# One activation table for Ln and Exp, loaded once ahead of the gated scan

## The chip, the cores and the metric

The kernel runs on one core of a Trainium2 chip. The metric is the device time of one execution in microseconds. Engines: TensorE (PE in the profile), VectorE (DVE), ScalarE (ACT), GpSimd (POOL) and SyncE (SP), each with an instruction stream of its own, in order; they wait for each other by semaphores.

## The reference

A complex gated linear recurrence over 768 steps, for 4 batches of 8 heads with 48 channels, and behind it a mixture of 8 experts in which each token takes one.

```python
mag = np.sqrt(a_re * a_re + a_im * a_im)
scale = np.minimum(mag, 0.999) / (mag + 1e-06)
a_re_n, a_im_n = (a_re * scale, a_im * scale)
for t in range(S):
    ar, ai = (a_re_n[:, :, t, :, None], a_im_n[:, :, t, :, None])
    kv = np.einsum('bhd,bhe->bhde', k[:, :, t], v[:, :, t])
    S_re, S_im = (ar * S_re - ai * S_im + kv, ar * S_im + ai * S_re)
    y[:, :, t] = np.einsum('bhd,bhde->bhe', q[:, :, t], S_re)
...
logits = x @ w_gate + modality_bias[modality_id]
e_idx = np.argmax(logits, axis=1)
out[mask] = gate_w[mask, None] * (np.maximum(x[mask] @ w1[e], 0.0) @ w2[e])
```

## The kernel before

The kernel has two parts. `gate_loop` computes the recurrence and the router's logits, `moe_sorted` (line 196 on) sorts the tokens by expert and computes the experts in 31 tiles of 128 tokens.

`gate_loop` cuts the 768 steps into 8 groups of L = 96 and puts (batch, head, group) on 128 partitions, so that the work comes in two rounds of two batches each (`NR = 2`). For each round there are two functions.

`elem(r)` works element by element, in 12 chunks of T = 8 steps, from the last step of a group to its first. A chunk loads the gates into `ab` (lines 65 and 66), squares them on ScalarE (L68), adds the squares on VectorE (L70), and turns the sum into the inverse magnitude by Ln (L72) and Exp (L73) on ScalarE. L75 (ScalarE) and L76 (VectorE) make the normalised gate's factor `g`, L79 (VectorE) with L80 and L81 (ScalarE) the table `an`, and L84 and L85 are the eight steps of the backward product of gates, each two VectorE instructions that depend on the ones before. From these products in `A`, ScalarE takes squares (L93), VectorE their sum (L95), ScalarE again Ln (L96) and Exp (L97). VectorE scales `q` by that (L98, L100) and `k` (L101); the scaled `k` goes to `kh` in DRAM (L102), the scaled `q` through eight transposes on TensorE (L106) into PSUM, and ScalarE copies them, four at a time, into `QT` (L107). The program interleaves neighbouring chunks: on each engine the second half of a chunk (L93 on) stands beside the first half of the next one (L68 to L81).

`units(r)` reads `kh` back as `KW` (L132) and runs the 8 groups in order, two batches each: transposes of `KW` and their copy (L139, L140), products with `QT` (L145) and a mask (L146), the outputs and the new state (L160, L164, L167, L169), copies of the output on ScalarE (L170, L171), the router's logits (L173, L182, L185, L186) and the rows of x (L176, L178, L180). The state is carried from group to group (L123 to L126, L150, L152).

The order on each engine is set by the tile framework's scheduler when the program is built, from `elem(0)`, `units(0)`, `elem(1)`, `units(1)`. It puts the first five chunks of `elem(1)` between the instructions of `units(0)`, and the rest behind them. `QT` has one buffer, so the copies L107 of round 1 come after `units(0)`.

No line of the kernel loads an activation table. A pass of the build puts a load (`ACT_TABLE_LOAD`) ahead of an ACTIVATE whose function is not in the table that is active at that place. Ln and Exp were given different tables by it, and so there is a load ahead of each: on lines 72, 73, 96 and 97, 24 times each, and one on line 68 for the first Square.

Of the kernel before, what the change touches and what calls it, by code (L numbers as in the profile page):

```python
# [22 lines left out]
def gate_loop(nc, ctx, tc, cpool, ident, identb, q, k, v, a_re, a_im, wgp, x_rows, lg):  # L23
# [86 lines left out]
    def units(r):  # L110
# [4 lines left out]
        for g in range(G):  # L115
# [70 lines left out]
            nc.scalar.copy(lg.rearrange("t (b g) e -> t b g e", g=G)[:, r * NB:(r + 1) * NB, g, :], lp[:])  # L186
            state = nstate.rearrange("p j (c d) -> p j c d", c=2)

    elem(0)
    for r in range(NR):  # L190
        units(r)
# [186 lines left out]
def kernel(  # L378
# [34 lines left out]
    with ExitStack() as gstack:  # L413
        gate_loop(nc, gstack, tc, cpool, ident, identb, q, k, v, a_re, a_im, wgp, x_rows, lg)
# [31 lines left out]
```

## Time and profile before

| | us |
|---|---|
| median of the 3 runs | 1039.46 |
| the runs | 1035.69 to 1046.57 |
| the profiled execution | 1047.4 |
| its span (first to last instruction) | 1045.7 |
| TensorE busy | 604.0 |
| ScalarE busy | 407.7 |
| VectorE busy | 377.9 |

The profile is of one execution, which took a little longer than the three timed runs. An engine's busy time is summed over its instructions, table loads among them; a share of the span says little here, since `elem` and `units` have different engines at work. So the stages are to be read one by one, and in each the wait that ends last. In a timeline a row has its start, its duration, the engine, line and operation, what is written from what, and in brackets how long the engine had been idle before it and who ended that.

### The profile page before, as it was taken

What the parts mean: (1) busy time and instruction counts of PE and PEld (TensorE: products, weight loads), DVE (VectorE), ACT (ScalarE), POOL (GpSimd) and SP (SyncE); (2) the same over time, 40 slices, a digit from 0 to 9 for tenths busy, and PEclk for the clock granted to TensorE, in tenths of its full rate; (3) what the DMA queues carried; (4) which work ended last, traced back from release to release, by engine and by line L of the source; (5) the groups of instructions that cost most, each with busy time, mean ns of one, the idle gap of its engine ahead of it and who ended that gap; (6) DMA issues with size and microseconds to landing.
All of it is one profiled execution on the core that took longest, in us unless ns stands there. A gap on an engine that the chain in (4) does not pass through costs nothing. (4 is left out here: it accounts for less than half of the span.)

```text
span 1045.7 us, 11696 instructions
## 1 busy us (share of the span) xinstructions
PE 604.0 (58%) x3599; PEld 385.7 (37%) x3599; DVE 377.9 (36%) x835; ACT 407.7 (39%) x716; POOL 82.8 (8%) x122
## 2 busy tenths in 40 slices
PE   0101010139987787010129999940479999999997
PEld 0101010126765565010116767730434444444443
DVE  3555555532555555646442243320511111111110
ACT  5566666632565667575732343320001111111111
POOL 0000000000000000000000000032032222222211
PEclk9999999999876667555555698675556656666556
DMA  3212121242353213212032243159910111111100
GB/s 93 91 45 90 46 87 49 81 98 71 82 124 99 53 45 115 69 53 84 30 85 67 69 97 76 43 80 207 202 34 32 35 34 35 35 35 34 28 4 1
DMA packets 104775, 71.58 MB, mean 68 GB/s; under 512 B 72878, under 2 KB 96930, under 8 KB 104720
## 3 DMA queue, kind: packets, MB, share of 16 engines
q0 software_dynamic: 14992, 20.36, 9.6%
q1 hardware_dynamic: 24768, 30.82, 9.5%
q10 hardware_dynamic: 64960, 19.67, 8.5%
q8 instruction: 35, 0.57, 0.2%
q14 instruction: 20, 0.16, 0.0%
HBM read 66.79 MB, written 17.99 MB: 81 GB/s over the span
## 5 line engine op out<-in xcount | busy, mean ns | idle before, releaser
L106 PE MATMUL tq<-ident,Qh 128*96 128x128 f32 x192 | 43.5, 403 | 313.2 <-DVE Qh L100 310.0
L363 PE MATMUL h_ps<-xgT,w1s 128*128 128x128 bf16 x744 | 169.4, 249 | 20.4 <-DVE xgT L356 14.5
L106 PEld LDWEIGHTS tq<-ident,Qh 128*96 128x96 f32 x192 | 32.8, 186 | 323.1 <-issue 315.1
L363 PEld LDWEIGHTS <-w1s 128*128 x744 | 76.4, 103 | 118.2 <-issue 42.6
L368 ACT ACTIVATE hT<-h_ps 128x512 bf16<-128x512 f32 x31 | 18.5, 598 | 235.9 <-PE h_ps L363 235.9
L160 PE MATMUL py<-KW,V 96*64 96x192 f32 x512 | 88.4, 430 | 6.2 <-issue 4.6
L146 DVE TENSOR_TENSOR KW<-wp,mask 96x384 f32<-96x384 f32 x64 | 35.3, 553 | 136.0 <-PE wp L145 135.2
L371 PE MATMUL y_ps<-w2s,hT 128*128 x248 | 83.7, 516 | 0.0
L145 PE MATMUL wp<-QT,KT 96*96 96x96 f32 x512 | 76.7, 319 | 3.9 <-ACT KT L140 3.9
L84 DVE TENSOR_TENSOR x<-A,an 128x192 f32<-128x192 f32 x192 | 68.6, 357 | 25.6 <-ACT an L81 19.9
L145 PEld LDWEIGHTS wp<-QT,KT 96*96 96x96 f32 x512 | 68.4, 226 | 14.1 <-ACT KT L140 7.4
L356 DVE COPY xgT<-xg_ps 128x384 bf16<-128x384 bf16 x31 | 11.1, 357 | 149.9 <-PE xg_ps L354 149.9
L133 POOL MEMSET V<- 96x128 f32 x32 | 6.4, 202 | 657.1 <-PE py L160 657.1
L93 ACT ACTIVATE sqe<-A 128x768 f32<-128x768 f32 x24 | 20.2, 843 | 95.2 <-DVE A L85 95.2
L366 DVE TENSOR_SCALAR hT<-h_ps 128x512 bf16<-128x512 f32 x31 | 21.4, 692 | 92.4 <-PE h_ps L363 92.4
L164 PE MATMUL py<-QT,Zs 96*48 96x96 f32 x448 | 51.8, 297 | 0.0
L85 DVE TENSOR_TENSOR A<-x 128x96 f32<-128x96 f32 x192 | 49.4, 257 | 6.4
L139 PE MATMUL tk<-ident,KW 96*96 96x96 f32 x256 | 44.1, 321 | 13.1 <-DMA KW<-kh 11.4
L160 PEld LDWEIGHTS py<-KW,V 96*64 96x64 f32 x512 | 43.5, 178 | 18.8 <-issue 14.1
L173 PE MATMUL lg_ps<-yT,wgp 128*8 128x96 f32 x256 | 41.1, 299 | 10.7 <-ACT yT L170 9.7
L371 PEld LDWEIGHTS <-hT 128*128 128x128 bf16 x248 | 35.4, 148 | 31.7 <-issue 31.3
L350 POOL DMA_INDIRECT xg<-x_rows,idg x31 | 30.3, 976 | 204.1 <-PE xg_ps L354 172.1
(119 smaller groups left out, 871.8 us busy)
## 6 DMA issues: line engine op xcount, KB each, us to landing
kh<-A SPq DMA_DIRECT2D x24, 384.0 KB, 2.6
KW<-kh ACTq DMA_DIRECT2D x32, 288.0 KB, 3.1
w1s<-in_moe_w_dram POOLq DMA_DIRECT2D x8, 768.0 KB, 27.4
w2s<-in_moe_w_dram POOLq DMA_DIRECT2D x8, 768.0 KB, 29.0
cB<-c_scr ACTq DMA_DIRECT2D x28, 192.0 KB, 3.9
V<-in_v_dram ACTq DMA_DIRECT2D x32, 144.0 KB, 2.5
ab<-in_a_re_dram SPq DMA_DIRECT2D x24, 192.0 KB, 2.9
ab<-in_a_im_dram SPq DMA_DIRECT2D x24, 192.0 KB, 3.2
```

The lines of the kernel that those rows point to most:

```text
L84: nc.vector.tensor_tensor(x[:], A[:, t + 1, :, None, :].broadcast_to([P, 2, 2, D]), an[:, t - t0].rearrange("p (u w) d -> p u w d", u=2), ...
L85: nc.vector.tensor_tensor(A[:, t], x[:, 0], x[:, 1], Alu.add)
L106: nc.tensor.transpose(tp[:, i, :], Qh[:, t4 + i].rearrange("p c d -> p (c d)"), ident[:])
L139: nc.tensor.transpose(tp[:, i, :], KW[:, h4 + i, 0:C], ident[:L, :L])
L145: nc.tensor.matmul(wp[:, i, :], KT[:, h4 + i, :], QT[:, p, :], start=True, stop=True)
L146: nc.vector.tensor_tensor(KW[:, h4:h4 + 4, C:], wp[:], mask[:, None, :].broadcast_to([L, 4, L]), Alu.mult)
L160: nc.tensor.matmul(py[u * 64:(u + 1) * 64, i, :], V[:, 2 * j + u, :], KW[:, 2 * j + u, :], start=True, stop=(g == 0))
L164: nc.tensor.matmul(py[u * 64:u * 64 + D, i, C:], Zs[:, j, u * 64:u * 64 + D], QT[:, p, :], start=False, stop=True)
L173: nc.tensor.matmul(lg_ps[:, b, :], wgp[:, j, :], yT[:, j, :], start=(j == 0), stop=(j == J - 1))
L350: nc.gpsimd.indirect_dma_start(out=xg[:], out_offset=None, in_=x_rows_dram, in_offset=bass.IndirectOffsetOnAxis(ap=idg[:, i:i + 1], axis=0))
L363: nc.tensor.matmul(h_ps[:, f, :], w1s[:, bass.ds(te, 1), k, ff * 128:(ff + 1) * 128], xgT[:, k, :], start=(k == 0), stop=(k == KD - 1))
L371: nc.tensor.matmul(y_ps[:], hT[:, f, :], w2s[:, bass.ds(te, 1), f, :], start=(f == 0), stop=(f == NF - 1))
```

## The change

One line is added ahead of `elem(0)`. It loads a table, by name, that holds Ln and Exp both. The lines behind it are numbered one higher in the kernel after.

```diff
@@ -186,6 +186,7 @@
             nc.scalar.copy(lg.rearrange("t (b g) e -> t b g e", g=G)[:, r * NB:(r + 1) * NB, g, :], lp[:])
             state = nstate.rearrange("p j (c d) -> p j c d", c=2)
 
+    nc.scalar.preload_act_table_set("natural_log_exp_and_others")
     elem(0)
     for r in range(NR):
         units(r)
```

The pass of the build takes account of the table that is active, so the program after has this one load and no other: 97 become 1. On TensorE, GpSimd and SyncE the order stays what it was. On ScalarE all other instructions keep their order too, but for one start of a transfer of `V` in the first chunk; on VectorE the cast of `identb` stands behind L79 of the first chunk instead of ahead of L76.

At the head of the program ScalarE has, before (`sq`, `ab`, `m` as in the lines above):

```order
L441 UNCONDITIONAL_BRANCH
L134 DMA V<-in_v_dram 96x8x48 x2
L68 ACT_TABLE_LOAD
L68 ACTIVATE sq<-ab 128x768
L72 ACT_TABLE_LOAD
L72 ACTIVATE m<-m 128x384
L73 ACT_TABLE_LOAD
L73 ACTIVATE m<-m 128x384
```

and after:

```order
L442 UNCONDITIONAL_BRANCH
L189 ACT_TABLE_LOAD
L134 DMA V<-in_v_dram 96x8x48 x2
L68 ACTIVATE sq<-ab 128x768
L72 ACTIVATE m<-m 128x384
L73 ACTIVATE m<-m 128x384
```

The load stands ahead of the starts of the transfers of `V`, and the Square no longer has one.

In the middle of `elem(0)`, from one chunk's squares of the products to the next chunk's copies into `an`, ScalarE has, before:

```order
L68 ACTIVATE sq<-ab 128x768
L96 ACT_TABLE_LOAD
L96 ACTIVATE me<-me 128x384
L97 ACT_TABLE_LOAD
L97 ACTIVATE me<-me 128x384
L72 ACT_TABLE_LOAD
L72 ACTIVATE m<-m 128x384
L73 ACT_TABLE_LOAD
L73 ACTIVATE m<-m 128x384
L75 ACTIVATE g<-m 128x384
L107 COPY QT<-tq 96x128x4 x2
L80 ACTIVATE an<-an 128x8x48
```

and after:

```order
L68 ACTIVATE sq<-ab 128x768
L96 ACTIVATE me<-me 128x384
L97 ACTIVATE me<-me 128x384
L72 ACTIVATE m<-m 128x384
L73 ACTIVATE m<-m 128x384
L75 ACTIVATE g<-m 128x384
L107 COPY QT<-tq 96x128x4 x2
L80 ACTIVATE an<-an 128x8x48
```

The four loads are gone, and the rest stands as it stood.

Where `elem(1)` lies between the instructions of `units(0)`, the loads stood ahead of copies for which TensorE waits (`yT`, L170). ScalarE at the first such place, before:

```order
L68 ACTIVATE sq<-ab 128x768
L96 ACT_TABLE_LOAD
L96 ACTIVATE me<-me 128x384
L97 ACT_TABLE_LOAD
L97 ACTIVATE me<-me 128x384
L132 DMA KW<-kh 96x8x96
L170 COPY yT<-py 128x192
L171 CAST yTb<-py 128x192
```

and after:

```order
L68 ACTIVATE sq<-ab 128x768
L96 ACTIVATE me<-me 128x384
L97 ACTIVATE me<-me 128x384
L132 DMA KW<-kh 96x8x96
L170 COPY yT<-py 128x192
L171 CAST yTb<-py 128x192
```

Two loads less stand ahead of L170.

## The prediction, made before the changed kernel ran

> **What bounds the kernel now.** I read the windows by stage first, then the groups of ScalarE by line, then the timeline of one chunk, and last the timeline of TensorE in the stage where the two parts of the scan overlap. The stages below are cut at the first load of `KW` of each round and at the last copy into `lg`; behind each stage's bounds and length stand the busy time (and instructions) of PE, PEld, DVE, ACT and POOL, the granted clock, the DMA share and GB/s.
>
> ```profile
> 0.00:223.60 223.60, 22.95 (x96) 17.36 (x96) 119.39 (x282) 138.65 (x184) 1.35 (x10) 1.00 0.24 74
> 223.60:405.00 181.40, 152.43 (x1131) 113.93 (x1132) 83.78 (x189) 93.19 (x203) 3.23 (x16) 0.77 0.33 80
> 405.00:541.60 136.60, 20.25 (x95) 15.12 (x93) 76.33 (x172) 87.92 (x120) 0.00 (x0) 0.52 0.22 70
> 541.60:691.70 150.10, 137.41 (x1128) 104.37 (x1128) 46.19 (x84) 51.01 (x146) 2.63 (x13) 0.74 0.29 69
> ```
>
> Rows one and three are `elem` alone (all of round 0, the last seven chunks of round 1 and a bit): ScalarE and VectorE are each busy a little over half the time and TensorE a seventh or less, so two engines wait for each other in turn. Row two is `units(0)` with five chunks of `elem(1)` between its steps, row four `units(1)` alone; both are TensorE's. What follows them, the experts, holds no table load before or after.
>
> ```profile
> L72 ACT ACT_TABLE_LOAD x24 | 30.8, 1283 | 0.4
> L73 ACT ACT_TABLE_LOAD x24 | 30.8, 1283 | 0.4
> L96 ACT ACT_TABLE_LOAD x24 | 30.8, 1283 | 0.4
> L97 ACT ACT_TABLE_LOAD x24 | 30.8, 1283 | 0.4
> L68 ACT ACT_TABLE_LOAD x1 | 1.3, 1283 | 5.5 <-DMA ab<-in_a_im_dram 5.5
> ```
>
> 97 loads of 1.283 us: 124.5 us of ScalarE. What each is worth depends on whether somebody waits for it. One chunk, in order of time (start, duration, engine, line; in brackets the idle time before it and who ended it):
>
> ```profile
> 19.21 0.84 ACT L93 ACTIVATE sqe<-A 128x768 f32<-128x768 f32 x1 [4.83 <-DVE A L85]
> ...
> 20.09 0.56 DVE L95 TENSOR_TENSOR me<-sqe 128x384 f32<-128x384 f32 x1 [0.23 <-ACT sqe L93]
> ...
> 20.82 0.56 DVE L70 TENSOR_TENSOR m<-sq 128x384 f32<-128x384 f32 x1 [0.17 <-ACT sq L68]
> 22.10 0.52 ACT L96 ACTIVATE me<-me 128x384 f32<-128x384 f32 x1
> ...
> 23.93 0.52 ACT L97 ACTIVATE me<-me 128x384 f32<-128x384 f32 x1
> 24.47 1.28 ACT L72 ACT_TABLE_LOAD   x1
> 24.49 0.56 DVE L98 TENSOR_TENSOR qc<-qc,me 128x384 f32<-128x384 f32 x1 [3.11 <-ACT me L97]
> 25.08 0.96 DVE L100 TENSOR_TENSOR Qh<-A,qc 128x768 f32<-128x768 f32 x1
> 25.77 0.52 ACT L72 ACTIVATE m<-m 128x384 f32<-128x384 f32 x1
> ...
> 26.18 1.91 PE L106 MATMUL tq<-ident,Qh 128*96 128x128 f32 x8 [26.18 <-DVE Qh L100]
> ...
> 27.60 0.52 ACT L73 ACTIVATE m<-m 128x384 f32<-128x384 f32 x1
> 28.16 0.52 ACT L75 ACTIVATE g<-m 128x384 f32<-128x384 f32 x1
> 28.58 1.05 ACT L107 COPY QT<-tq 96x512 f32<-96x512 f32 x2
> 28.71 0.56 DVE L76 SCALAR_TENSOR_TENSOR g<-m,g 128x384 f32<-128x384 f32 x1 [2.67 <-ACT g L75]
> ...
> 30.05 0.95 DVE L79 TENSOR_TENSOR an<-ab,g 128x768 f32<-128x768 f32 x1
> ...
> 31.04 0.52 ACT L80 ACTIVATE an<-an 128x384 f32<-128x384 f32 x1 [1.41 <-DVE an L79]
> 31.47 0.51 ACT L81 ACTIVATE an<-an 128x384 f32<-128x384 f32 x1
> ...
> 32.01 0.36 DVE L84 TENSOR_TENSOR x<-A,an 128x192 f32<-128x192 f32 x1 [1.00 <-ACT an L81]
> ...
> 36.80 0.84 ACT L93 ACTIVATE sqe<-A 128x768 f32<-128x768 f32 x1 [4.82 <-DVE A L85]
> ```
>
> The reader is to see a closed loop. From L93 to the second copy of L107 ScalarE has no idle time at all, and four loads stand in that stretch; VectorE waits 3.11 us for L97 and 2.67 us for L75 meanwhile. Then VectorE makes `an`, ScalarE its two copies, VectorE the eight steps of the scan, and those release the next L93, 17.59 us after the first. Nothing else runs in the loop that could take over the loads' place: they are on the path.
>
> **The change, part by part.** *Four loads gone from a chunk of elem alone.* I count the loop again from L93 = 0. L68 starts 0.75 us later as before (its 0.83 us end at 1.58, and L70, which waits for it, starts at 1.61). L95 is over at 1.44 (20.09 + 0.56 - 19.21), so L96 can start at 1.5. A dependent pair without a load between is L73 and L75: 28.16 - 27.60 = 0.56. An independent pair is L80 and L81: 31.47 - 31.04 = 0.43. So L97 starts at 2.06, L72 at 2.49 (L70 is over at 2.17), L73 at 3.05, L75 at 3.61, and g is there at 4.13 instead of 9.47 (28.16 + 0.52 - 19.21). On VectorE L98 starts at 2.61, L100 at 3.20 and ends at 4.16, so L76 starts at 4.2 and L79 1.34 later (30.05 - 28.71), at 5.54; by that L80 could start at 6.53 (0.99 after L79) where it was at 11.83. What is late next is L107: it stands ahead of L80 on ScalarE and its second copy needs the eighth transpose, which ended 3.01 us after L100's start (26.18 + 1.91 - 25.08). Now that is 3.20 + 3.01 = 6.21, the copy starts at about 6.25 and L80 half a copy-pair (1.05 / 2) later, at 6.75. Gain 11.83 - 6.75 = 5.08 us of 17.59: about the four loads (5.13), the smaller losses and gains cancelling. The new period is 12.5 us.
>
> How many such chunks: the first and last L93 of round 0 and those of the undisturbed part of round 1 are
>
> ```profile
> 212.70 0.84 ACT L93 ACTIVATE sqe<-A 128x768 f32<-128x768 f32 x1 [4.82 <-DVE A L85]
> 425.97 0.84 ACT L93 ACTIVATE sqe<-A 128x768 f32<-128x768 f32 x1 [4.83 <-DVE A L85]
> 531.50 0.84 ACT L93 ACTIVATE sqe<-A 128x768 f32<-128x768 f32 x1 [4.82 <-DVE A L85]
> ```
>
> (212.70 - 19.21) / 17.59 = 11 periods and (531.50 - 425.97) / 17.59 = 6. Seventeen periods at 5.08 us: 86.4 us.
>
> *The ends of these stretches.* Round 0's first chunk:
>
> ```profile
> 5.47 1.28 ACT L68 ACT_TABLE_LOAD   x1 [5.47 <-DMA ab<-in_a_im_dram]
> 7.64 0.56 DVE L70 TENSOR_TENSOR m<-sq 128x384 f32<-128x384 f32 x1 [6.44 <-ACT sq L68]
> 8.92 0.52 ACT L72 ACTIVATE m<-m 128x384 f32<-128x384 f32 x1
> ```
>
> The load of L68 goes to the head, inside the 5.47 us that ScalarE waits for `ab`: 1.28 us. L72's load was half covered by L70, which ends 0.72 us before L72 starts: 0.7 us. L73's is bare: 1.28. Sum 3.3 us. The last chunk of round 0 saves the loads of L96 and L97, 2.6 us; the load of L72 behind them is covered by the transposes and the `kh` transfer. The last chunk of round 1 has no L68, so L96 waits for L95 and 2.0 us remain. The chunk that starts `elem` alone in round 1 (405 to 426) also empties eight held-back copies of L107, which hide a little: four loads, 4.8 us. Together 12.7 us.
>
> *Seventeen loads inside units(0).* ScalarE has idle time there, so a load counts only where TensorE or VectorE then waits for it. The five longest times that TensorE stood for ScalarE in this stage:
>
> ```profile
> 289.54 0.50 PE L173 MATMUL lg_ps<-yT,wgp 128*8 128x96 f32 x4 [2.52 <-ACT yT L170]
> 333.34 0.81 PE L173 MATMUL lg_ps<-yT,wgp 128*8 128x96 f32 x4 [2.63 <-ACT yT L170]
> 356.81 0.81 PE L173 MATMUL lg_ps<-yT,wgp 128*8 128x96 f32 x4 [3.10 <-ACT yT L170]
> 363.97 2.88 PE L145 MATMUL wp<-QT,KT 96*96 96x96 f32 x16 [1.32 <-ACT KT L140]
> 387.89 2.88 PE L145 MATMUL wp<-QT,KT 96*96 96x96 f32 x16 [1.66 <-ACT KT L140]
> ```
>
> Ahead of each ScalarE ran two loads with their ACTIVATEs, 2.57 us of loads, in front of the copy that TensorE wanted. The sum is 11.2 us and I take 11: most of each wait is load. The bounds are 0 (VectorE's share of the chunk, which stays, holds TensorE just as long) and all seventeen, 21.8 us.
>
> *The added load.* One, at the head, in front of two starts of `V` transfers that nobody needs before `units(0)`; ScalarE waits for `ab` then anyway. Cost nothing; were `ab` there at once, 1.28 us. The cast of `identb` moves behind L79, into VectorE's 1.00 us wait for L81: nothing.
>
> **Sum**: 86.4 + 12.7 + 11 = 110 us. The profiled execution took 1047.4 us (span 1045.7) and becomes 937; the median of the runs shown is 1039.46, and 110 off that is 929.
>
> [...] A load that stands between a dependent pair costs 27.60 - 25.77 = 1.83 against 0.56 without, so 1.27; between an independent pair 25.77 - 23.93 = 1.84 against 0.43, so 1.41. [...]
>
> **The rivals.**
> 1. *units(0) gives nothing.* Its loads hide behind TensorE, or VectorE's steps of the chunk take the place of the waits. For it: row two has VectorE busy 83.78 us against 46.19 in units(1). Against: the five waits name ScalarE. Gain 99, time 936 to 944.
> 2. *units(0) gives more.* Fewer pauses let TensorE's clock stay up (the same four matmuls of L173 take 0.50 us at 289.54 and 0.81 at 333.34). At most units(0) comes down to units(1), 181.4 - 150.1 = 31 us: time 905 to 922. [...]
> 3. *Another link of the chunk takes over.* Each microsecond that the second L107 waits longer for the transposes costs 17 us. With one to two of them the gain is 76 to 93 and the time 946 to 963. Against: the transposes take in round 1, at half the granted clock, what they take at 26.18:
>
> ```profile
> 537.81 1.91 PE L106 MATMUL tq<-ident,Qh 128*96 128x128 f32 x8 [14.94 <-DVE Qh L100]
> ```
>
> 4. *A switch holds more than its load.* If every pair behaved like the independent one, the 80 loads outside units(0) would give 0.13 us more each: 10 us, 919. Against: three of the four loads of a chunk stand in front of an ACTIVATE that has to wait for the one before it or for VectorE. [...]
> 5. *The other side: Ln and Exp run slower from the table that holds both.* The place is those 96 ACTIVATEs, most of them on the loop. Break-even is 110 / 96 = 1.15 us more each, 1.67 us instead of 0.52; from 1.8 us the kernel is slower by over 1%. Against: Ln, Exp and the Copy of L75 come from two tables now and take 0.52 each. That loads remain is out: the built order has one.
>
> **How the numbers follow.** Forecast (units(0) gives 4 to 18): 0.64, its own range 922 to 936. Rival 1: 0.12. Rival 2: 0.15. Rival 3: 0.05. Rival 4: 0.02. Rival 5: 0.02, half of it within 1%. The predicted time is 929. The range 913 to 944 holds the forecast, rival 1 and half of rival 2, 0.83, and the runs' own spread of about 5 us either way lies in it. 1% is about what a measurement of this kernel can tell from no change. Faster by over 1%: 0.98; within: 0.01; slower: 0.01.
>
> **What would show it.** In the profile after: one ACT_TABLE_LOAD; L93 to L93 in `elem` 12.5 us; VectorE's wait for L97 under 1.5 us; L107 with a wait for TensorE where it had none; the first load of `KW` at 162 us instead of 223.6; the units(0) stage 170 us long and the stretch to the next `KW` 100; units(1) and the experts as before. A period over 14 us, or Ln and Exp not at 0.52 us, would make the prediction wrong.

## The result, and the profile after

| | before | after |
|---|---|---|
| median of 4 runs, us | 1037.68 | 918.68 |
| the runs, us | 1035.69 to 1046.57 | 908.7 to 921.5 |
| the profiled execution, us | 1047.4 | 921.5 |

The ratio is 0.8821, with a 95% interval of 0.8733 to 0.8909. The kernel is 119 us faster by the medians; the two profiled executions are 126 us apart. The ratios and intervals, here and below, leave out executions over 1.5% slower than the fastest of the same kernel.

The stages of the kernel after, cut at the same instructions as before (bounds and length, then busy time of PE, PEld, DVE, ACT and POOL with the instructions, granted clock, DMA share, GB/s):

```profile
0.00:162.29 162.29, 22.95 (x96) 17.43 (x96) 118.49 (x282) 74.36 (x135) 1.35 (x10) 1.00 0.33 101
162.29:317.38 155.09, 137.66 (x1131) 103.51 (x1132) 83.06 (x189) 70.75 (x186) 3.22 (x16) 0.87 0.39 94
317.38:416.29 98.91, 18.61 (x96) 13.88 (x93) 75.72 (x173) 48.54 (x90) 0.00 (x0) 0.55 0.31 96
416.29:566.43 150.14, 137.59 (x1128) 104.42 (x1128) 46.21 (x84) 50.94 (x146) 2.62 (x13) 0.74 0.30 69
```

Against the rows of before, `elem(0)` lost 61.3 us, `units(0)` 26.3, the rest of `elem(1)` 37.7, and `units(1)` nothing. In the two stages of `elem` alone VectorE's busy time is what it was, ScalarE's fell by the loads, and both stages shrank by nearly as much as that. The row for the one load that is left, in the groups of ScalarE by line:

```profile
L189 ACT ACT_TABLE_LOAD x1 | 1.3, 1283 | 0.8 <-PEq L431 0.8
```

One chunk of `elem` alone, in order of time, answers to the chunk shown before:

```profile
66.27 0.84 ACT L93 ACTIVATE sqe<-A 128x768 f32<-128x768 f32 x1 [4.82 <-DVE A L85]
...
67.75 0.51 ACT L96 ACTIVATE me<-me 128x384 f32<-128x384 f32 x1
...
68.29 0.52 ACT L97 ACTIVATE me<-me 128x384 f32<-128x384 f32 x1
68.72 0.51 ACT L72 ACTIVATE m<-m 128x384 f32<-128x384 f32 x1
68.84 0.56 DVE L98 TENSOR_TENSOR qc<-qc,me 128x384 f32<-128x384 f32 x1 [0.41 <-ACT me L97]
69.26 0.52 ACT L73 ACTIVATE m<-m 128x384 f32<-128x384 f32 x1
...
69.81 0.52 ACT L75 ACTIVATE g<-m 128x384 f32<-128x384 f32 x1
70.38 0.55 DVE L76 SCALAR_TENSOR_TENSOR g<-m,g 128x384 f32<-128x384 f32 x1
...
71.71 0.58 ACT L107 COPY QT<-tq 96x512 f32<-96x512 f32 x1 [1.38 <-PE tq L106]
71.72 0.95 DVE L79 TENSOR_TENSOR an<-ab,g 128x768 f32<-128x768 f32 x1
...
72.56 0.58 ACT L107 COPY QT<-tq 96x512 f32<-96x512 f32 x1 [0.27 <-PE tq L106]
...
73.04 0.52 ACT L80 ACTIVATE an<-an 128x384 f32<-128x384 f32 x1
...
78.80 0.84 ACT L93 ACTIVATE sqe<-A 128x768 f32<-128x768 f32 x1 [4.82 <-DVE A L85]
```

The loop closes after 12.53 us where it took 17.59. VectorE's wait for L97 is 0.41 us where it was 3.11, and for L75 it no longer waits. ScalarE, which had no idle time up to L107, now waits there 1.38 and 0.27 us for the transposes, and L80 comes right behind the second copy: 1.32 us after L79's start, where 0.99 would do.

Inside `units(0)`, the waits of TensorE for ScalarE's copies (total us, times, longest), first of the kernel before and then of the kernel after:

```profile
PE lg_ps L173 <- ACT yT L170: 9.1, 5, 3.1
PE wp L145 <- ACT KT L140: 3.0, 2, 1.7
```

```profile
PE lg_ps L173 <- ACT yT L170: 2.6, 6, 0.6
PE wp L145 <- ACT KT L140: 0.5, 2, 0.3
```

Nine microseconds of waits went there. The stage lost 26.3 us, though, and most of the rest is in the first number of its row: TensorE's busy time for the same 1131 matmuls was 152.43 us and is 137.66. The same matmuls ran faster. That is what the experiments had to explain.

### The profile page after: what moved, and what is told of

Same layout as the page of the kernel before. It is cut to its first block, busy times and chain, and to the rows that moved or that the text cites. A ratio compares the mean times of both kernels' runs of the same rounds, so it can differ in the third digit from the quotient of the medians.

```text
span 919.8 us, 11601 instructions
## 1 busy us (share of the span) xinstructions
PE 586.6 (64%) x3599; PEld 373.8 (41%) x3599; DVE 375.7 (41%) x835; ACT 281.5 (31%) x620; POOL 82.6 (9%) x122
## 5 line engine op out<-in xcount | busy, mean ns | idle before, releaser
L160 PE MATMUL py<-KW,V 96*64 96x192 f32 x512 | 84.4, 414 | 5.1 <-issue 4.1
L145 PEld LDWEIGHTS wp<-QT,KT 96*96 96x96 f32 x512 | 66.5, 220 | 11.7 <-ACT Zs L152 4.9
L164 PE MATMUL py<-QT,Zs 96*48 96x96 f32 x448 | 49.0, 286 | 0.0
L93 ACT ACTIVATE sqe<-A 128x768 f32<-128x768 f32 x24 | 20.2, 843 | 94.0 <-DVE A L85 94.0
L139 PE MATMUL tk<-ident,KW 96*96 96x96 f32 x256 | 40.6, 302 | 12.6 <-DMA KW<-kh 11.2
L160 PEld LDWEIGHTS py<-KW,V 96*64 96x64 f32 x512 | 41.4, 171 | 17.3 <-issue 12.6
L173 PE MATMUL lg_ps<-yT,wgp 128*8 128x96 f32 x256 | 38.4, 283 | 4.4 <-ACT yT L170 3.2
```

The lines of the kernel that those rows point to most:

```text
L139: nc.tensor.transpose(tp[:, i, :], KW[:, h4 + i, 0:C], ident[:L, :L])
L145: nc.tensor.matmul(wp[:, i, :], KT[:, h4 + i, :], QT[:, p, :], start=True, stop=True)
L160: nc.tensor.matmul(py[u * 64:(u + 1) * 64, i, :], V[:, 2 * j + u, :], KW[:, 2 * j + u, :], start=True, stop=(g == 0))
L164: nc.tensor.matmul(py[u * 64:u * 64 + D, i, C:], Zs[:, j, u * 64:u * 64 + D], QT[:, p, :], start=False, stop=True)
L173: nc.tensor.matmul(lg_ps[:, b, :], wgp[:, j, :], yT[:, j, :], start=(j == 0), stop=(j == J - 1))
```

## The experiments

Theory A is that the loads' own time is all there is to the change: a load costs what it keeps somebody waiting, and in `units(0)` its pauses of TensorE also bring the matmuls' clock down. Its rivals are named in each expectation.

Five of the kernels put loads back into the kernel after, each of the one table that is active anyway, so that nothing but the time of a load is added. `reload_at` does that in the order that the scheduler has made: it sets a load directly ahead of the given ones of a line's ACTIVATEs or copies, counted from 0, and leaves all others in place. The load itself carries no semaphore. Where a wait stands ahead of a copy as an instruction of its own, the load comes behind that wait.

### All loads back, of one table

```diff
     with _tile.TileContext(nc) as tc:
         tile_gateloop__then__limoe_modality_prior_kernel(tc, *args)
+    reload_at(nc, {L72: range(24), L73: range(24), L96: range(24), L97: range(24)})
```

> The kernel after, with the 96 loads back where they stood, but all of the one table that is active already. Theory A (the gain is the loads' time and nothing else: 1.283 us each, no cost of the switch of functions and no faster ACTIVATE): the time is that of before, 1038, within 6 us; chunk period of elem 17.6 us (only the first chunk gains, 1.3 us). Rival B (two tables cost more than their loads, or the one table's Ln and Exp are faster): well below before; with 0.13 us for each of 80 loads 10 us below, 1028, and a period of about 17.1.

Measured: 1038.81 us against 1039.38 of before on the same chip, ratio 0.9973 (0.9929 to 1.0016). The period of the chunk is back, by two neighbouring L93 of its timeline:

```profile
71.20 0.84 ACT L93 ACTIVATE sqe<-A 128x768 f32<-128x768 f32 x1 [4.82 <-DVE A L85]
88.79 0.84 ACT L93 ACTIVATE sqe<-A 128x768 f32<-128x768 f32 x1 [4.82 <-DVE A L85]
```

17.59 us. Loading one table again and again is as slow as going to and fro between two (the interval leaves at most 7 us), so the gain comes from the loads' time. Neither the other table for Ln and Exp nor the switch of functions shows a share. Rival B falls: it wanted a period of 17.1 and a time of 1028.

### Only the loads inside units(0)

```diff
+    reload_at(nc, {L72: range(13, 17), L73: range(12, 17), L96: range(12, 16), L97: range(12, 16)})
```

> The kernel after, with only the 17 loads back that stood inside units(0). In the two profiles so far that stage fell from 181.4 to 155.1 us, where the prediction had 11 us. Theory A (the loads caused all of it: 11 us of pauses of TensorE, and 15 us of a lower clock that followed from the pauses): stage 181, time 919 + 26 = 945. Rival C (the 15 us are chance, how the clock's windows fell in the two profiled executions): stage about 166, time 930.

Measured: 947.06 us, ratio to before 0.907 (0.8999 to 0.9141); the kernel after took 924.84 beside it. The stage:

```profile
162.18:345.12 182.94, 154.89 (x1131) 115.17 (x1132) 83.83 (x189) 93.12 (x203) 3.22 (x16) 0.79 0.33 79
```

182.94 us long, as before (181.40), with TensorE's busy time back at 154.89; all other stages stay at their lengths of the kernel after. TensorE's waits for `yT` are back too:

```profile
PE lg_ps L173 <- ACT yT L170: 8.0, 5, 2.5
```

So these seventeen loads alone bring both, the pauses and the slower matmuls. Rival C, chance for the whole 15 us, falls: it wanted 930 us.

### Only the loads outside units(0)

```diff
+    reload_at(nc, {L72: [*range(13), *range(17, 24)], L73: [*range(12), *range(17, 24)],
+                   L96: [*range(12), *range(16, 24)], L97: [*range(12), *range(16, 24)]})
```

> The complement: the 79 loads back that stood outside units(0), none inside. Theory A: elem periods of 17.6 us, units(0) stays at 155, time 919 + 98 = 1017. Rival C: units(0) scatters between 155 and 170 from run to run; time 1017 to 1032.

Measured: 1020.35 us, ratio to before 0.9734 (0.963 to 0.9838). In its profile the period is 17.6 us, and `units(0)` is short:

```profile
222.64:379.40 156.76, 136.33 (x1131) 103.19 (x1132) 83.16 (x189) 71.29 (x186) 3.23 (x16) 0.88 0.38 92
```

Without the inner loads 19 us are gained against before, an interval of 1.6 to 3.7%; without the outer ones 92. Together that is 111 of the 115 us by which the kernel after beat the kernel before in the same set of runs, so the two halves add up.

### The kernel after once more

No edit.

> The kernel after, unchanged, a second profile. Theory A: units(0) again 155 us within 4, clock there 0.85 or more, time 908 to 922. Rival C: units(0) takes 160 to 170 us in this execution.

Measured: 924.84 us (910.48 to 927.82), 3 above the expected times. In its profile `units(0)` took 156.9 us at a granted clock of 0.87, with a busy TensorE of 137.5.

### Loads where ScalarE waits anyway, in elem

```diff
+    reload_at(nc, {L93: [*range(1, 12), *range(17, 24)]})
```

> The kernel after, with 18 loads added in elem alone, one a chunk, directly ahead of L93, where ScalarE waits 4.82 us for VectorE. Theory A (a load costs what it keeps somebody waiting): nothing, period 12.53 us and the time of the kernel after, 909 to 928. Rival D (a load has its price wherever it stands): 18 x 1.28 = 23 us more, about 943.

Measured: 917.17 us, ratio 0.8825 (0.8754 to 0.8896); the kernel after beside it had 916.12. The end of a chunk in its timeline (L423 is the load):

```profile
61.16 0.51 ACT L81 ACTIVATE an<-an 128x384 f32<-128x384 f32 x1
...
61.69 1.28 ACT L423 ACT_TABLE_LOAD   x1
61.70 0.36 DVE L84 TENSOR_TENSOR x<-A,an 128x192 f32<-128x192 f32 x1 [1.33 <-ACT an L81]
...
66.50 0.84 ACT L93 ACTIVATE sqe<-A 128x768 f32<-128x768 f32 x1 [3.53 <-DVE A L85]
```

The load fills part of the wait for VectorE, which shrinks from 4.82 to 3.53 us, and the period stays at 12.54 (the next L93 starts at 79.04). The same instruction that costs 1.28 us ahead of L96 costs nothing ahead of L93. Rival D falls.

### Loads where ScalarE waits anyway, in units(0)

```diff
+    reload_at(nc, {L140: [0], L167: [0, 2, 3], L178: [0, 2],
+                   L170: [4, 5, 6, 8, 9, 17, 20, 21], L152: [0, 1, 8]})
```

> The kernel after, with 17 loads added inside units(0), as many as before, but ahead of copies for which ScalarE had waited 1.3 us or more in the kernel after. ScalarE is as busy as before there. Theory A (what counts are the pauses of TensorE, and its clock follows them): units(0) 155 to 160 us, granted clock there 0.85 or more, time 919 to 925. Rival E (the occupied ScalarE itself, wherever the loads stand, or chance): units(0) 170 to 182, clock 0.8, time 935 to 947.

Measured: 920.98 us, ratio 0.8875 (0.8813 to 0.8937). The stage:

```profile
162.17:318.34 156.17, 136.87 (x1131) 103.39 (x1132) 83.46 (x189) 92.87 (x203) 3.22 (x16) 0.80 0.38 93
```

ScalarE is as busy as with the loads at their old places (92.87 against 93.12 us), yet the stage takes 156.17 us and TensorE's matmuls 136.87. So it isn't the occupied ScalarE, but whom it keeps waiting. TensorE's waits for `yT` stay short here:

```profile
PE lg_ps L173 <- ACT yT L170: 3.8, 9, 0.6
```

Rival E falls. Two limits are to be kept in mind. Thirteen of these loads run in the first 51 us of the stage, where the old places begin at 41 us. And two of them, at 211.68 and 250.66, started only when TensorE had ended ScalarE's wait, so they did hold up their copies, but cost TensorE no more than 0.6 us. One part of the expectation failed: the granted clock is 0.80, not 0.85. The busy time of the same matmuls shows that they ran as fast as in the kernel after all the same (the last section tells why the two figures differ).

### The copies of the transposes later

```diff
-                nc.scalar.copy(QT[:, :, t0 + t4:t0 + t4 + 4], tp.rearrange("c t p -> c p t"))
+                late.append((tp, t0 + t4))
...
-            nc.scalar.activation(an[:, :, 3, :], an[:, :, 0, :], Act.Copy)
+            last = nc.scalar.activation(an[:, :, 3, :], an[:, :, 0, :], Act.Copy)
+            with tc.issue_after(last.ins):
+                while late:
+                    tp, at = late.pop(0)
+                    nc.scalar.copy(QT[:, :, at:at + 4], tp.rearrange("c t p -> c p t"))
```

(What is in `late` after the last chunk of a round is copied ahead of L108.)

> The kernel after, with the two copies of L107 behind L81 in ScalarE's order instead of ahead of L80. Theory A (the second copy, which waits for the eighth transpose, now holds L80): L80 starts 0.99 us after L79 instead of 1.32, period 12.53 - 0.33 = 12.2 us, 17 x 0.33 = 5.6 us off the time of the kernel after. Rival F (L80 waits for VectorE as long as for L107, or something else ends last): period 12.5, time as the kernel after.

> The kernel after, unchanged, as the measure for the three runs beside it: units(0) 155 to 158 us, time 909 to 928.

Measured: 910.97 us (ratio 0.8758, 0.8694 to 0.8822) against 916.12 for the kernel after (0.8862, 0.8793 to 0.8931). The kernel after's `units(0)` took 152.4 us in this profile, below the expected 155 to 158. Both kernels were timed again, in more runs:

> The copies of L107 behind L81 once more, timed longer beside the kernel after: a period of 12.2 us and a time 5.6 us below the kernel after of the same chip if the two links of the chunk are all that differs; the same time if what the chunk gains is given back in units(0) or units(1).

> The kernel after, unchanged, as the measure for the run beside it: period 12.53 us, units(0) 152 to 158 us, time 909 to 928.

Measured: 905.63 us (0.8707, 0.8673 to 0.8741) against 918.78 (0.8747, 0.8699 to 0.8796). The chunk in the second profile; lines are numbered higher there, L80, L81 and L82 are the old L79, L80 and L81, L86 is the copy and L98 the old L93:

```profile
70.50 0.95 DVE L80 TENSOR_TENSOR an<-ab,g 128x768 f32<-128x768 f32 x1
71.49 0.52 ACT L81 ACTIVATE an<-an 128x384 f32<-128x384 f32 x1 [2.38 <-DVE an L80]
71.92 0.51 ACT L82 ACTIVATE an<-an 128x384 f32<-128x384 f32 x1
72.33 1.05 ACT L86 COPY QT<-tq 96x512 f32<-96x512 f32 x2
...
77.25 0.84 ACT L98 ACTIVATE sqe<-A 128x768 f32<-128x768 f32 x1 [3.87 <-DVE A L90]
...
89.45 0.84 ACT L98 ACTIVATE sqe<-A 128x768 f32<-128x768 f32 x1 [3.87 <-DVE A L90]
```

The old L80 starts 0.99 us after L79, and the period is 12.20 us, in both profiles of this kernel: the 0.33 us that was expected. The second copy of L107 was what held the chunk in the kernel after, and rival F falls. Seventeen periods and the end pieces shorten the two stages of `elem` to 158.8 and 96.9 us, 5.5 us less than in the kernel after. In the time the intervals of the two kernels still overlap. Over the executions of both sets that count in the ratios, nine and six, the means are 906.6 and 912.1 us, 5.5 apart (95%: 1 to 10), which agrees with the expected 5.6. Of the kernels here this one has the lowest time.

## Why the prediction was right, point by point

The predicted 929 us lies 10 above the measured median, and the range held the measured time. That time, 919, is 3 us below the forecast's own range, though, and among the times of rival 2: the range held it only because half of that rival was taken in. The larger part, the loads outside `units(0)`, came as forecast.

- *Four loads of a chunk are on the path.* Right. The period was forecast as 12.5 and is 12.53; L80 stands 6.77 us behind L93 (73.04 - 66.27), forecast 6.75.
- *L107 is late next.* Right, by the trace and by the two runs that moved it.
- *The ends of the stretches.* Right: the first `KW` was forecast at 162 and its load started at 162.29; the stretch to the next at 100 and took 98.91. Together the loads outside `units(0)` gave 99.0 us (61.3 + 37.7) of the forecast 99.
- *Seventeen loads inside units(0): 11 us.* The waits were right, the size was not. This is the term that was mis-sized: it measured 26 us in the two profiles, and the stage was 155 us long where the prediction's signs had 170. The 11 us that the prediction counted in waits are there: the stage's time in which TensorE ran no matmul fell from 29 us (181.4 - 152.4) to 17.4. (Its list of the five longest waits for ScalarE lacks one, 1.52 us of L185 for L182 at 385.18.) What it left out of the sum, and had as rival 2 with a chance of 0.15, is the matmuls' speed.
- *The added load and the moved cast.* Right, nothing: the load runs from 0.82 us on, while `ab` is on its way.
- *Rivals 1, 3, 4 and 5.* Out. Rival 1 wanted nothing from `units(0)`. Rival 3 wanted a longer period than 12.5. Rival 4 wanted more than the loads' time, and the loads of one table gave all of it. For rival 5 Ln and Exp would have to be slower, and they take 0.51 to 0.52 us each, as before.

The stage in the profiles of all the kernels whose program there is the same but for the loads (rest is the time in which TensorE ran no matmul):

| units(0), us | length | TensorE busy | rest |
|---|---|---|---|
| loads at the old places: before | 181.4 | 152.4 | 29.0 |
| all loads back | 174.4 | 145.1 | 29.3 |
| only those of units(0) | 182.9 | 154.9 | 28.1 |
| no loads: after | 155.1 | 137.7 | 17.4 |
| after, second | 156.9 | 137.5 | 19.5 |
| after, third | 152.4 | 132.0 | 20.4 |
| after, fourth | 156.3 | 136.5 | 19.9 |
| only the loads outside units(0) | 156.8 | 136.3 | 20.4 |
| loads in elem's idle time | 153.0 | 132.6 | 20.4 |
| loads in units(0)'s idle time | 156.2 | 136.9 | 19.3 |

The means of the two groups, three rows with the loads at their old places and seven without, are 179.6 and 155.2 us: 24 us less, of them 15.2 in TensorE's busy time and 9.2 beside it. The groups don't overlap in any of the three columns.

That the clock follows from the pauses is what the runs support: seventeen loads that make no long pause (waits for `yT` of at most 0.6 us) bring no slower matmuls (136.9 us), as many at their old places bring both (up to 2.5 us, and 154.9 us). It isn't shown for all of the 15.2 us. The first long wait that the loads make ends 66 us into the stage. Ahead of its matmul TensorE is busy 54.3 to 55.9 us with the loads and 47.0 to 55.9 without, and 3.4 us of the difference of the means lie there, where no such pause can have caused them. Behind it are the other 11.8 us, and there the groups just touch (89.2 to 100.6 and 78.3 to 89.7). Pauses without any load on ScalarE were not tried, so the clock's own rule was not measured. In each of the profiles with the slower matmuls three waits of 2.2 to 3.1 us went along with them, beside two that all ten profiles have: 5.9 to 6.9 us for the first `KW`, and 1.6 to 2.7 us further on.

## What to carry to other kernels

Functions of ScalarE that alternate on a dependent path belong in one table: on this path each load was worth 1.27 of its 1.28 us ((17.59 - 12.53) / 4), and the same load in a wait was worth nothing, so look at who waits behind it before counting. Where a stage is TensorE's, a stall of another engine that makes it pause may cost more than the pause (here seventeen loads cost the stage 24 us, 9.2 of them without a matmul); put the matmuls' busy time before and after beside the waits. And after such a gain look for the link that holds the loop next: here it was a copy in the queue ahead of the ACTIVATE that the loop needed.

## What the runs showed of the hardware that had not been expected

- The seventeen loads, 21.8 us of ScalarE, were worth 24 us of the stage in the profiles and 19 and 22 us by the medians of the runs. That is about their whole time, though only 9 us of it are pauses of TensorE; the rest is slower matmuls.
- `units(1)` holds no load in any of these kernels, and its length still went from 139.2 to 150.9 us from profile to profile, by TensorE's busy time alone (126.1 to 138.0). Of the 13.0 us between the third and the fourth profile of the kernel after, 909.0 and 922.0 us long, `units(1)` makes 8.7 (141.8 and 150.5).
- The granted clock of a stage can mislead: before its first record of the execution it counts as 1.00. So `elem(0)` shows 1.00, though eight transposes take 1.91 us there as in the stage that shows 0.52 (both in the kernel before). And `units(0)` showed 0.80 in one profile and 0.87 in another with nearly the same busy time for the same matmuls (136.9 and 137.7 us): the first record comes at 177.7 us in the one and at 203.7 in the other. In the traces of before and after the records hold 0.50 and 1.00 alone, and the first is one of 1.00, at 264.1 and 203.7 us. With half clock up to the first record, `units(0)` comes to an estimated 0.66 before (0.77 shown), 0.73 after (0.87 shown) and 0.75 with the loads in its idle time (0.80 shown).
